# Chunks 2 to 21 of a chunked linear-attention kernel put in the order of a list schedule made at build time

## The chip, the cores and the metric

The kernel runs on one NeuronCore of a Trainium2 chip. The metric is the device time of one execution in microseconds (us); the time given for a kernel is the median of its runs. The engines are called PE (TensorE; PEld is its weight load), DVE (VectorE), ACT (ScalarE), POOL (GpSimd) and SP (SyncE, which here only issues DMAs). Each engine works off its own instructions in the order in which the program holds them; between engines there are semaphore waits, which the framework sets wherever two instructions touch the same data.

## The reference

For each of 4 x 8 heads a 40x40 state is carried over 768 steps, and its output, 3072 tokens of 320 numbers, goes through a mixture of experts with a skip gate:

```
for t in range(S):
    y[:, :, t] = einsum('bhd,bhde->bhe', rt, state)
    Sa = einsum('bhde,bhe->bhd', state, at)
    state_decay = state * wt[:, :, None, :] - einsum('bhd,bhe->bhde', Sa, bt)
    state = state_decay + einsum('bhd,bhe->bhde', vt, kt)
...
do_compute = x @ w_skip > 0                  # other tokens: out = x
e_idx = argmax(xc @ w_gate); gate_w = softmax(...)[e_idx]
out[do_compute] = xc + gate_w * (relu(xc @ w1[e]) @ w2[e])
```

## The kernel before

The sequence is cut into 24 chunks of 32 steps. The 32 heads lie in two halves, x = 0 and x = 1, of 16 heads each. Within a chunk the recurrence is solved with matrices; between chunks only the 40x40 states are carried. The chunk loop in `attn` writes out, for each chunk c, the steps below in an order made by hand, and PE, ACT and DVE keep that order (`tc.manual_schedule`); POOL and SP are ordered by the framework, except in the prologue, where POOL is kept too.

The chain from chunk to chunk, for each half x, is:

- `rs` (L288): 16 small matmuls of r with the state, copied out by DVE (L292, even chunks) or ACT (L293, odd ones);
- `ux` (L302): matmuls of the chunk's decayed a with R1, copied to `UXs` by ACT (L304);
- `uq` (L313): matmuls with the inverse `TB`, four ACT copies into R1 (L315), and a mask on POOL (L317);
- `sst` (L325, L330): two sets of matmuls that make the new state and its transpose, copied by DVE (L334) or ACT (L335), and ACT (L338).

Beside the chain stand:

- `yy` (L348): the chunk's output, scaled by DVE into `XS` (L352) and stored twice by SP (L353);
- the preparation of later chunks, in units of a pair of chunks h. The scans on DVE (L114, L126, L119), products on POOL (L143, L151), the matrices in `m1` (L163: PE; L165: ACT copy; L174: DVE transpose; L170: POOL mask; L172: four DMAs on SP), and the transposes `kbt` (L185, L188), `wtt` (L197, L199) and `m2` (L207, L209);
- `tinv`, the inverse of 32x32 triangles for the next four chunks: 30 steps of two products (L228) and two subtractions (L230) on DVE, half of them on a block that lies in PSUM (`px`), then an ACT copy (L232) and a DVE transpose into `TB` (L235). `T()` puts one or two of its steps between the other steps of a chunk;
- the routing of the finished tokens (`route`), two chunks at a time: transposes on PE (L628), ACT copies (L630), scores (L636, L637), a row of small DVE operations (L644 to L681) with one exponential on ACT between L646 and L653, and scattered stores on POOL (L684). `RP(...)` says at which places of a chunk it goes on one step;
- the loads on SP of w, a, k/b and v (L94, L97, L100, L107) and on POOL of r/v (L104).

Scans, `m1` and `tinv` run in chunks 0 to 19; chunks 20 to 23 only finish. The loads of the experts' weights begin in chunk 20, the experts themselves follow the last chunk.

The eight PSUM banks are dealt out in fixed rings: two banks `pc` (for `rs`, `ux`, `uq`), two `ps` (`sst`), two `pq` (all preparation and routing), one `py` (`yy`), one `px` (`tinv`). A ring gives its banks in turn:

```
    def tile(s,shape,dt,tag=None,name=None):
        t=s.t[s.n%len(s.t)]; s.n+=1
```

Of the kernel before, what the change touches and what calls it, by code (L numbers as in the profile page):

```python
# [19 lines left out]
def host(r,k,v,w,a,b,moe_w_skip,moe_w_gate,moe_w1,moe_w2):  # L20
# [16 lines left out]
    o.update(raw_r=r,raw_k=k,raw_v=v,raw_w=w,raw_a=a,raw_b=b)  # L37
    o.update(moe_host(moe_w_skip,moe_w_gate,moe_w1,moe_w2))
    return o
class Ring:  # L40

    def __init__(s,pool,n,k):
        s.t=[pool.tile([128,512],F32,name=f"{n}{q}") for q in range(k)]; s.n=0
    @classmethod
    def of(c,t):
        r=c.__new__(c); r.t=t; r.n=0
        return r
    def tile(s,shape,dt,tag=None,name=None):
# [9 lines left out]
def attn(ctx,tc,i,m,out,X):  # L58
    nc=tc.nc; NPH=6
    ov=out.rearrange("(b c t) f -> c b t f",b=4,t=32); Xv=X.rearrange("(b c t) f -> c b t f",b=4,t=32)  # L60
    P=lambda n,b,**k: ctx.enter_context(tc.tile_pool(name=n,bufs=b,**k))
    cp=P("const",1); wk=P("wk",1); wk2=P("wk2",2); wk3=P("wk3",3); wk4=P("wk4",4)
# [297 lines left out]
    if 1:  # L360
# [248 lines left out]
KT=((0,128),(128,256),(256,320))  # L609
class Moe:  # L610
    def __init__(s,ctx,tc,i,out,cp):
        s.tc,s.nc,s.i,s.out=tc,tc.nc,i,out; s.ctx=ctx
        nc=tc.nc
        dr=ctx.enter_context(tc.tile_pool(name="dr",bufs=1,space=DRAM))
        s.xg=dr.tile([E_*CAP,XW],F32,name="xg")
        s.X=dr.tile([3072,DM],F32,name="X")
        s.mc=cp.tile([128,552],F32,name="mc")
        s.wg=cp.tile([128,3,9],F32,name="wg")
        tz=s.mc[:,488:552]; s.mT=bass.AP(tz.tensor,tz.offset+31,(tuple(tz.ap[0]),(-1,32),(1,32))); s.mQ=s.mc[:,32:64]; s.idn=s.mc[:,64:192]; s.tri=s.mc[:,192:320]; s.one=s.mc[:,320:448]
        s.e8=s.mc[:,448:456]; s.base0=s.mc[:,456:464]; s.tok=s.mc[:,464:488]  # L620
        s.base=s.base0; s.WH,s.WL={},{}
# [226 lines left out]
                V.tensor_tensor(S,S,g,ALU.add)  # L848
            for b in range(4): nc.sync.dma_start(xv[b][:,ds(t0,U),:],y[8*b:8*b+8])
def dense_moe(m,X):  # L850
    tc,nc=m.tc,m.nc; V=nc.vector
    with tc.tile_pool(name="gw",bufs=1) as wp, tc.tile_pool(name="gps",bufs=1,space=PSUM) as gps:
        m.ps,m.wk=gps,wp
        with tc.For_i(0,3072,128) as r0:
# [12 lines left out]
                V.copy_predicated(acc,mk,y)  # L867
            nc.sync.dma_start(m.out[ds(r0,128),:],acc)
def general(m,fi,raw,X):
    tc,nc=m.tc,m.nc  # L870
    fa=nc.values_load(fi[0:1,2:3],min_val=0,max_val=1)
    fw=nc.values_load(fi[0:1,0:1],min_val=0,max_val=1)
    with tc.If(fa>0):
        with tc.If(fw>0):
            seq_attn(tc,raw,X)
        dense_moe(m,X)

def build(tc,i,out):
    with ExitStack() as ctx:
# [8 lines left out]
        with tc.manual_schedule(engines={ET.PE,ET.Activation,ET.DVE}), P("pp",1,space=PSUM) as m.pp, P("rt",1) as m.wk, P("xp",2) as m.xp:  # L888
# [16 lines left out]
```

## Time and profile before

| | us |
|---|---|
| median of 3 runs (666.47 to 667.10) | 666.92 |
| the profiled execution | 663.83 |
| its span, first to last instruction | 662.1 |
| chunk 2's first `rs` to chunk 22's first `rs` | 97.16 to 487.45 |
| start of the experts' steady part (stage from 530) to the end | 132 |

Times within the trace count from the start of the span. The stages of the prediction are cut at the first `rs` matmul (L288) of chunks 2, 4, 8, 12, 16, 20 and 22. In a row of the timeline stand start, duration, engine, line, operation, `output<-input`, shapes, a count, and in brackets the engine's idle time ahead of it and the instruction that ended it. In a list of waits stand who waited for whom, the total in us, how often, and the longest.

### The profile page before, as it was taken

The page shows a single profiled execution, that of the slowest core. Times are in us where ns is not written, and L with a number is a line of the kernel's source. Part 1 is how long each engine was busy: PE and PEld are TensorE (multiplying, and loading weights), DVE is VectorE, ACT ScalarE, POOL GpSimd, SP SyncE. Part 2 cuts the span into 40 slices and gives each one's busy share as a digit, 9 for nine tenths or more (in the row PEclk, how much of TensorE's full clock was granted, in tenths as well). Part 3 has the DMA queues.
Part 4 walks back from the last instruction along what each step waited for, and adds up shares of the span by engine and source line. Part 5 has one row for each costly group of instructions (what it writes and reads, how often), then busy time and mean ns, then how long its engine had stood idle before and what let it go on. Part 6 is the DMA issues. An engine that isn't in the chain of part 4 may idle for free.

```text
span 662.1 us, 33508 instructions
## 1 busy us (share of the span) xinstructions
PE 515.5 (78%) x14772; PEld 432.2 (65%) x14772; DVE 489.7 (74%) x1182; ACT 419.5 (63%) x1151; POOL 324.2 (49%) x246
## 2 busy tenths in 40 slices
PE   4777776676776787767785877878886899999995
PEld 1543456565664576656664666666775599999995
DVE  7998697858997479973999736864166457888881
ACT  5463674586965778567785677887885354555540
POOL 5481951648545375553946442223132155666661
PEclk8786895799977898878889689988788999999998
DMA  7473665352443525335253333453365266676210
GB/s 227 152 242 107 166 207 160 104 177 63 139 125 107 174 63 150 109 112 168 83 156 88 107 113 81 140 153 113 105 178 167 73 183 201 214 229 216 77 48 24
DMA packets 67446, 91.06 MB, mean 138 GB/s; under 512 B 32564, under 2 KB 54657, under 8 KB 65806
## 3 DMA queue, kind: packets, MB, share of 16 engines
q1 hardware_dynamic: 62350, 74.05, 38.1%
q0 software_dynamic: 4944, 14.80, 6.6%
q8 instruction: 118, 1.93, 1.2%
q14 instruction: 34, 0.28, 0.1%
HBM read 74.03 MB, written 17.08 MB: 138 GB/s over the span
## 4 chain that ended last, share of the span: by engine, by line
PE 24%; DVE 11%; ACT 8%; issue 5%; DMA 2%; POOL 1%; SPq 0%; POOLq 0%; DVEq 0%; ACTq 0%
PE pc L782 5%; PE ps L793 4%; PE px L782 3%; ACT R1t L315 2%; PE py L793 2%; ACT L2t L188 2%; DVE M L228 2%; PE ps L325 2%; DVE ti L789 2%; PE pc L313 1%; PE pc L288 1%; DVE M L230 1%; PE ps L330 1%; ACT SS L338 1%; ACT R1t L209 1%
## 5 line engine op out<-in xcount | busy, mean ns | idle before, releaser
L317 POOL TENSOR_TENSOR R1t<-R1t,mc 64x512 f32<-64x512 f32 x46 | 60.5, 1315 | 104.7 <-ACT R1t L315 72.6
L315 ACT COPY R1t<-pc 32x288 f32<-32x288 f32 x192 | 74.9, 390 | 20.7 <-PE pc L313 17.6
L730 POOL TENSOR_TENSOR WL<-WR,WH 128x1280 fp32r<-128x1280 f32 (+1 forms) x21 | 57.7, 2782 | 8.7 <-ACT WH L729 8.6
L188 ACT COPY L2t<-pq 64x160 f32<-64x160 f32 x184 | 52.8, 287 | 7.5 <-PE pq L185 5.1
L684 POOL DMA_INDIRECT xg<-XS,ix x24 | 25.5, 1064 | 64.3 <-DMA xg<-XS,ix 26.0
L325 PE MATMUL ps<-R1t,L2t 128*40 128x40 f32 x1472 | 48.2, 221 | 11.0 <-issue 5.3
L143 POOL TENSOR_TENSOR WR<-WR,M 128x1024 f32<-128x1024 f32 (+1 forms) x19 | 44.2, 2332 | 25.8 <-DVE M L114 19.7
L228 DVE TENSOR_TENSOR M<-M 128x22 f32<-128x22 f32 (+10 forms) x110 | 55.0, 500 | 0.0
L325 PEld LDWEIGHTS ps<-R1t,L2t 128*40 128x40 f32 x1472 | 39.3, 132 | 18.9 <-ACT R1t L315 8.9
L338 ACT COPY SS<-ps 40x320 f32<-40x320 f32 x92 | 38.7, 420 | 19.9 <-PE ps L330 18.5
L209 ACT COPY R1t<-pq 32x128 f32<-32x128 f32 x184 | 47.2, 256 | 5.5 <-PE pq L207 1.3
L288 PE MATMUL pc<-rvt,SS 128*40 128x32 f32 x1472 | 44.9, 216 | 7.2 <-issue 4.8
L288 PEld LDWEIGHTS pc<-rvt,SS 128*40 128x40 f32 x1472 | 38.3, 135 | 15.4 <-issue 7.8
L330 PE MATMUL ps<-L2t,R1t 128*40 128x40 f32 x1472 | 42.9, 218 | 6.5 <-issue 6.4
L313 PE MATMUL pc<-UXs,TB 32*32 32x72 f32 x1536 | 43.1, 255 | 6.0 <-issue 5.9
L330 PEld LDWEIGHTS ps<-L2t,R1t 128*40 128x40 f32 x1472 | 38.2, 134 | 7.3 <-issue 7.2
L230 DVE TENSOR_TENSOR M<-M 128x22 f32<-128x22 f32 (+10 forms) x110 | 40.8, 371 | 0.0
L230 DVE TENSOR_TENSOR px<-px,M 128x168 f32<-128x168 f32 (+8 forms) x150 | 39.1, 260 | 1.4
L729 ACT CAST WH<-WR 128x1024 fp32r<-128x1024 f32 (+1 forms) x35 | 39.6, 1132 | 0.0
L313 PEld LDWEIGHTS pc<-UXs,TB 32*32 32x32 f32 x1536 | 32.1, 122 | 11.4 <-issue 8.9
L789 DVE CAST ti<-xe 128x2 int32<-128x2 f32 x8 | 39.3, 4911 | 0.2
L174 DVE STREAM_TRANSPOSE M<-pq 128x128 f32<-128x128 f32 x40 | 12.1, 308 | 36.9 <-ACT M L165 24.3
(240 smaller groups left out, 1529.3 us busy)
## 6 DMA issues: line engine op xcount, KB each, us to landing
rvt<-rv POOLq DMA_DIRECT2D x21, 512.0 KB, 3.9
WR<-kb SPq DMA_DIRECT2D x10, 1024.0 KB
WR<-w SPq DMA_DIRECT2D x16, 640.0 KB
WR<-w SPq DMA_DIRECT2D x16, 512.0 KB
M<-wt SPq DMA_DIRECT2D x9, 520.5 KB
M<-at SPq DMA_DIRECT2D x8, 512.0 KB
WR<-w SPq DMA_DIRECT2D x16, 256.0 KB
R1t<-vt SPq DMA_DIRECT2D x48, 80.0 KB
```

Source lines behind the costliest of these rows:

```text
L188: A.copy(L2[x][h%NL2][64-64*x:128-64*x,c,bb*4:bb*4+4,:],pt[64*c:64*c+64,:,64*x:64*x+40])
L209: A.copy(R1[x][c%NR1][ao[x]:ao[x]+32,4*b:4*b+4,40:72],Pp[32*b:32*b+32])
L228: V.tensor_tensor(tv,NLt[:,j,j+1:32].unsqueeze(2).broadcast_to([128,n,k]),X[:,j,lo:hi].unsqueeze(1).broadcast_to([128,n,k]),ALU.mult)
L230: for tv,xv in q: V.tensor_tensor(xv,xv,tv,ALU.subtract)
L288: TE.matmul(RS[s,v,:],SS[x][:,b//2,v,:],rr[:,b%2,2*hh+x,:],start=True,stop=True)
L313: TE.matmul(UQ[q,hh,:],Tb[q,x*8+hh*2+c%2,:],UXd[x][q,hh,:],start=True,stop=True)
L315: A.copy(R[uu,4*b:4*b+4,:],UQ[32*b:32*b+32,:,:])
L317: (V if c==NC-1 else G).tensor_tensor(R[pq,:,40:72],R[pq,:,40:72],mQ[pq].unsqueeze(1).broadcast_to([64,16,32]),ALU.mult)
L325: TE.matmul(ST[s,v,:],l2[:,cc,u,:],R[:,u,0:40],start=True,stop=True)
L330: TE.matmul(S2[s,v,:],R[:,u,0:40],l2[:,cc,u,:],start=True,stop=True)
L730: def low(s,E,o,x,h): E.tensor_tensor(s.R(o),x,h,ALU.subtract)
L782: for n,(a,b) in enumerate(mm): TE.matmul(ph[:,g],R(a),R(b),start=n==0,stop=n==7)
```

## The change

All engines are wrapped (`Eng`, `Rec`). From chunk 2 on (`rec.on=True`) no instruction is issued; each call is kept as a task, with the data that it reads and writes (down to the partition quarter and the element), a cost in us from a formula by engine and size, and a latency for DMAs. Consecutive matmuls into one PSUM tile are one task. At chunk 22 `rec.flush()` finds the dependences, makes a list schedule of all tasks of chunks 2 to 21 on DVE, ACT, POOL, PE and SP, and issues the tasks by their planned start. POOL's order is kept in that stretch as well. The list takes, on each engine, the task with the smallest key (place in the old order less the weighted length of the work that hangs on it) among those that are ready, unless another one fits in before it.

The six banks of `pq`, `pc` and `ps` become one stock: a tile in PSUM gets its bank in the plan. The two banks `ps` are kept for `sst` and for the oldest tile that waits. Of the banks that are free in time the plan takes the one that became free last. `py` and `px` stay as they are. Small tiles that a pool gave out in turn become fixed tiles in turn with the same number of buffers (`Static`).

What is computed, the number of instructions of each engine and the code of one chunk are the same; chunks 0, 1, 22 and 23, the prologue and the experts are issued as before. The other edits touch the fallback path for unusual inputs, which does not run.

The core of the diff:

```
+class Rec:
+    HOP=0.12; PW=1.25
+    def cost(s,e,op,w,r,a):
+        n=max(sz(x) for x in (w[:1]+r[:1]))
+        if 'dma' in op:
+            by=4*n*min(128,w[0].ap[0][1])
+            return (0.06 if e=='S' else 1.0 if 'ind' in op else 0.6),2.0+by/2.6e5
+        if e=='P': return (0.145 if op=='transpose' else max(0.0005*sz(w[0]),0.058)),0
+        if e=='A': return 0.15+0.00085*n,0
+        if e=='G': return (0.08+n*0.0008 if op=='memset' else 0.65+0.0015*n),0
...
+        if op=='tensor_tensor': return 0.14+0.00105*n*(1 if ps else 1.6),0
...
+    def plan(s,keep=False):
...
+                av=[(at[k],k) for k in at if at[k] is not None and k not in got.values() and (k not in s.rest or o==old[0] or s.first[o] in s.rest)]
+                if not av: return None
+                a=max(min(av)[0],free[T[i].e],rdy[i])
+                a,k=max(x for x in av if x[0]<=a)
...
+                c.sort(key=lambda x:s.key[x[1]])
+                x=c[0]
+                while True:
+                    f=[y for y in c if y[0]<x[0] and y[0]+T[y[1]].d<=x[0]+s.LET]
+                    if not f: break
+                    x=f[0]
...
+    def keys(s):
+        w=max(sum(t.d for t in s.tasks if t.e==e) for e in 'VAGP')/len(s.tasks)
+        s.key=[i*w-s.FAR*t.up for i,t in enumerate(s.tasks)]
...
-    ps_c,ps_s,ps_y,ps_p,ps_x=(Ring(pp,n,k) for n,k in (("pc",2),("ps",2),("py",1),("pq",2),("px",1))); m.ps=ps_p
+    rec.banks={t.name:t for t in PQ+PC+PS}; rec.rest=[t.name for t in PS]
+    ps_c,ps_s,ps_p=(Ring(t,rec) for t in (PC,PS,PQ)); ps_y,ps_x=Ring(PY),Ring(PX); m.ps=ps_p
...
+            if c==2: rec.on=True
             if c==20: m.load(0)
             if c==22:
+                with tc.manual_schedule(engines={ET.Pool}): rec.flush()
```

Two places of the engines' orders follow. The changed kernel issues everything from one helper, so that its rows have one line number, L209; the operands tell what a row is. Banks are numbered: pq, pc and ps have two each, and the numbers behind the names differ between the two kernels.

**DVE, chunk 11, the end of the third inversion.** `M<-M,px` and `px<-px,M` are the last steps of `tinv`, `XS<-py` the output of a chunk, `TB<-M` the transpose that ends the inversion, `R1t<-ps` the new state. Before:

```order
L228 TENSOR_TENSOR M<-M,px_106 128x8
L230 TENSOR_TENSOR px_106<-px_106,M 128x8
L352 TENSOR_TENSOR XS<-py_103,WT 128x320
L235 STREAM_TRANSPOSE TB<-M 128x32x2x2x8
L334 TENSOR_TENSOR R1t<-ps_102,D_2599 40x8x40 x2
```

And now:

```order
L209 TENSOR_TENSOR M<-M,px_106 128x8
L209 STREAM_TRANSPOSE M<-pc_101 128x4x32
L209 TENSOR_TENSOR px_106<-px_106,M 128x8
L209 STREAM_TRANSPOSE M<-ps_103 128x4x32
L209 STREAM_TRANSPOSE M<-pq_99 128x4x32
L209 STREAM_TRANSPOSE M<-ps_104 128x4x32
L209 MEMSET M 128x17
L209 TENSOR_TENSOR XS_1345<-py_105,WT_478 128x320
L209 STREAM_TRANSPOSE TB<-M 128x32x2x2x8
L209 SCALAR_TENSOR_TENSOR M<-M 128x1041
```

Three transposes of `m1` and a memset, which belong to other work, now stand with the output's product between the last subtraction and the transpose into `TB`; with the one ahead of them the transposes empty four different banks.

**PE, chunks 2 and 3, around the routing's transposes.** `pq<-WR` (32x64) is `m1`, `mc,XS` the routing's transpose of a chunk's output, `rvt,SS` is `rs`, `UX,TB` is `uq`, `R1t,WR` or `R1t,M` is `ux`, `rvt` alone `m2`, `L2t,R1t` and `R1t,L2t` (40x40) are `sst`. Before:

```order
L163 MATMUL pq_104<-WR 32x64 x16
L302 MATMUL pc_99<-R1t,M 32x72 x16
L207 MATMUL pq_105<-rvt 32x32 x16
L628 MATMUL pq_104<-mc,XS 128x128 x2
L628 MATMUL pq_104<-mc,XS 64x128
L288 MATMUL pc_100<-rvt,SS_116 40x32 x16
```

And now:

```order
L209 MATMUL pq_99<-WR 32x64 x16
L209 MATMUL pc_102<-UX_451,TB 32x72 x16
L209 MATMUL pq_100<-rvt_150,SS_116 40x32 x16
L209 MATMUL pc_101<-WR 32x64 x16
L209 MATMUL pc_102<-rvt_150 32x32 x16
L209 MATMUL ps_104<-mc,XS_1344 128x128 x2
L209 MATMUL ps_104<-mc,XS_1344 64x128
L209 MATMUL pq_100<-WR 32x64 x16
L209 MATMUL ps_103<-L2t,R1t 40x40 x16
L209 MATMUL pc_102<-R1t,WR 32x72 x16
L209 MATMUL ps_104<-wg,xT_1466 32x9 x12
L209 MATMUL pc_102<-R1t,L2t 40x40 x16
```

Before, the routing's transpose went into the bank that an `m1` two groups ahead had filled; now it takes a bank that no `m1` holds, two such products stay in banks of their own, and one bank (`pc_102`) is filled four times in eleven rows.

More of the change, by code (lines that the diff above doesn't have):

```diff
@@ L39, in host, with __init__, __getattr__, tile @@
     return o
+class Task:
+    __slots__=("e","op","calls","R","W","d","lat","out","p","n","pr","al","up")
+class Eng:
+    def __init__(s,rec,e,real): s.rec,s.e,s.real=rec,e,real
+    def __getattr__(s,op):
+        fn=getattr(s.real,op)
+        return lambda *a,**k: s.rec.call(s.e,op,fn,a,k)
+class Shim: pass
+class Static:
+    def __init__(s,pool,bufs): s.pool,s.bufs,s.r=pool,bufs,{}
+    def tile(s,shape,dt,tag=None,name=None,bufs=None):
+        t=tag or name; n=int(np.prod(shape[1:]))
+        if t not in s.r: s.r[t]=[[s.pool.tile([128,n],dt,name=f"{t}{q}") for q in range(bufs or s.bufs)],0]
+        r=s.r[t]; x=r[0][r[1]%len(r[0])][0:shape[0],0:n]; r[1]+=1
+        if len(shape)==2: return x
+        ax=["abcd"[q] for q in range(len(shape)-1)]
+        return x.rearrange("p ("+" ".join(ax)+") -> p "+" ".join(ax),**{a:v for a,v in zip(ax,shape[1:])})
@@ L40, with __init__, of @@
 class Ring:
-    def __init__(s,pool,n,k):
-        s.t=[pool.tile([128,512],F32,name=f"{n}{q}") for q in range(k)]; s.n=0
+    def __init__(s,t,rec=None): s.t=t; s.n=0; s.rec=rec
     @classmethod
-    def of(c,t):
-        r=c.__new__(c); r.t=t; r.n=0
-        return r
+    def of(c,t,rec=None): return c(t,rec)
     def tile(s,shape,dt,tag=None,name=None):
         t=s.t[s.n%len(s.t)]; s.n+=1
+        if s.rec: s.rec.bank(t)
         n=int(np.prod(shape[1:]))
@@ L60, in attn @@
     ov=out.rearrange("(b c t) f -> c b t f",b=4,t=32); Xv=X.rearrange("(b c t) f -> c b t f",b=4,t=32)
-    P=lambda n,b,**k: ctx.enter_context(tc.tile_pool(name=n,bufs=b,**k))
-    cp=P("const",1); wk=P("wk",1); wk2=P("wk2",2); wk3=P("wk3",3); wk4=P("wk4",4)
+    P=lambda n,b,**k: Static(ctx.enter_context(tc.tile_pool(name=n,bufs=1,**k)),b)
+    rec=m.rec; nc=rec.shim
+    cp=P("const",1).pool; wk=P("wk",1); wk2=P("wk2",2); wk3=P("wk3",3); wk4=P("wk4",4)
     pp=m.pp
-    ps_c,ps_s,ps_y,ps_p,ps_x=(Ring(pp,n,k) for n,k in (("pc",2),("ps",2),("py",1),("pq",2),("px",1))); m.ps=ps_p
+    bk=lambda n,k: [pp.tile([128,512],F32,name=f"{n}{q}") for q in range(k)]
+    PQ,PC,PS,PY,PX=bk("pq",2),bk("pc",2),bk("ps",2),bk("py",1),bk("px",1)
+    rec.banks={t.name:t for t in PQ+PC+PS}; rec.rest=[t.name for t in PS]
+    ps_c,ps_s,ps_p=(Ring(t,rec) for t in (PC,PS,PQ)); ps_y,ps_x=Ring(PY),Ring(PX); m.ps=ps_p
     V,A,G,TE,SP=nc.vector,nc.scalar,nc.gpsimd,nc.tensor,nc.sync
@@ L611, in __init__ @@
     def __init__(s,ctx,tc,i,out,cp):
-        s.tc,s.nc,s.i,s.out=tc,tc.nc,i,out; s.ctx=ctx
+        s.rec=Rec(tc.nc); s.tc,s.nc,s.i,s.out=tc,s.rec.shim,i,out; s.ctx=ctx
         nc=tc.nc
@@ L850, in dense_moe @@
 def dense_moe(m,X):
-    tc,nc=m.tc,m.nc; V=nc.vector
+    m.nc=m.tc.nc; tc,nc=m.tc,m.nc; V=nc.vector
     with tc.tile_pool(name="gw",bufs=1) as wp, tc.tile_pool(name="gps",bufs=1,space=PSUM) as gps:
@@ L869, in general @@
 def general(m,fi,raw,X):
-    tc,nc=m.tc,m.nc
+    tc,nc=m.tc,m.tc.nc
     fa=nc.values_load(fi[0:1,2:3],min_val=0,max_val=1)
@@ L887, in build @@
         P=lambda n,b,**k: tc.tile_pool(name=n,bufs=b,**k)
-        with tc.manual_schedule(engines={ET.PE,ET.Activation,ET.DVE}), P("pp",1,space=PSUM) as m.pp, P("rt",1) as m.wk, P("xp",2) as m.xp:
+        with tc.manual_schedule(engines={ET.PE,ET.Activation,ET.DVE}), P("pp",1,space=PSUM) as m.pp, P("rt",1) as rt, P("xp",1) as xp:
+            m.wk,m.xp=Static(rt,1),Static(xp,2)
             with ExitStack() as c2: attn(c2,tc,i,m,out,m.X)
```

122 lines of the change are left out of this document (added).

## The prediction

> **What bounds the kernel now.** I read the page first, for what ends last:
>
> ```profile
> span 662.1 us, 33508 instructions
> PE 515.5 (78%) x14772; PEld 432.2 (65%) x14772; DVE 489.7 (74%) x1182; ACT 419.5 (63%) x1151; POOL 324.2 (49%) x246
> PE 24%; DVE 11%; ACT 8%; issue 5%; DMA 2%; POOL 1%; SPq 0%; POOLq 0%; DVEq 0%; ACTq 0%
> ```
>
> No engine is full, and the chain goes through three of them. A mean over the span mixes stages, so the busy times of the stages come next, cut at the first `rs` matmul of chunks 2, 4, 8, 12, 16, 20 and 22:
>
> ```profile
> core 0: us, PE busy (x) PEld busy (x) DVE busy (x) ACT busy (x) POOL busy (x), PEclk, DMA share, GB/s
> 0.00:97.16 97.16, 66.26 (x1789) 41.60 (x1789) 83.61 (x132) 54.20 (x146) 57.59 (x50) 0.84 0.59 179
> 97.16:143.86 46.70, 32.72 (x1188) 27.71 (x1179) 36.38 (x110) 29.20 (x90) 20.79 (x17) 0.78 0.47 143
> 143.86:224.14 80.28, 57.76 (x2245) 47.58 (x2236) 66.10 (x184) 57.82 (x176) 45.66 (x36) 0.89 0.42 123
> 224.14:305.95 81.81, 60.72 (x2247) 50.42 (x2237) 64.10 (x184) 57.80 (x176) 43.26 (x36) 0.85 0.42 120
> 305.95:386.91 80.96, 60.26 (x2245) 49.72 (x2236) 65.54 (x184) 57.73 (x176) 45.75 (x36) 0.87 0.42 125
> 386.91:454.84 67.93, 52.78 (x2119) 44.45 (x2109) 43.44 (x170) 53.79 (x164) 18.09 (x18) 0.92 0.42 121
> 454.84:487.45 32.61, 28.12 (x1004) 23.49 (x995) 7.26 (x28) 27.13 (x83) 8.37 (x8) 0.84 0.39 116
> 530.00:662.00 132.00, 123.19 (x936) 121.31 (x936) 96.16 (x108) 60.33 (x81) 73.42 (x37) 0.98 0.48 149
> ```
>
> The changed stretch is 97.16 to 487.45, 390.29 us for 20 chunks. DVE is the busiest engine up to chunk 15, ACT in chunks 16 to 19, PE in 20 and 21, with shares of 78, 82, 78, 81, 79 and 86%. The busiest engines' times add up to 36.38 + 66.10 + 64.10 + 65.54 + 53.79 + 28.12 = 314.03 us, or 80.5% of the stretch. The other 76 us are waits in an order made by hand. Which ones, the waits of DVE in the stretch tell:
>
> ```profile
> DVE M L174 <- ACT M L165: 24.3, 8, 6.4
> DVE mx L644 <- ACT sc L637: 21.8, 6, 9.3
> DVE TB L235 <- ACT M L232: 13.9, 5, 3.0
> DVE sm L653 <- ACT ex L647: 10.8, 7, 3.1
> ```
>
> These 70.8 us are of one kind: an instruction for later use (a transpose of `m1`, a routing step, the end of an inversion) stands at the head of the queue before its input is there, and what is behind it could run. Two examples from the timeline:
>
> ```profile
> 302.99 1.97 DVE L235 STREAM_TRANSPOSE TB<-M 128x1024 f32<-128x1024 f32 x1 [2.84 <-ACT M L232]
> 314.58 0.32 DVE L174 STREAM_TRANSPOSE M<-pq 128x128 f32<-128x128 f32 x1 [5.23 <-ACT M L165]
> ```
>
> PE has the same through the banks. Here, in the timeline, the routing's transpose waits until DVE empties the bank of an `m1`:
>
> ```profile
> 125.71 0.90 PE L628 MATMUL pq<-mc,XS 128*128 128x128 f32 x3 [4.14 <-DVE M L174]
> ```
>
> And in the waits of PE over the stretch the same wait and two others for a bank of that ring:
>
> ```profile
> PE pq L628 <- DVE M L174: 12.3, 5, 4.1
> PE pq L207 <- ACT L2t L188: 10.8, 9, 1.4
> PE pq L185 <- ACT L2t L188: 5.2, 8, 1.6
> ```
>
> **The change part by part.** *The order.* No computing instruction is added or taken away: by the two orders each engine has as many as before (PE 8327, DVE 1316, ACT 1192, POOL 270, SP 400). So busy times stay, and only waits can change. At the first place shown in the change, the inversion's last transpose has three other transposes and a memset between it and its input; at the second, the routing's transpose no longer shares a bank with an `m1`. Both waits quoted from there should shrink or go.
>
> How full can the busiest engine get? From below, the nearest row is chunks 20 and 21: the same steps in the same in-order queues, with little preparation between them, PE at 28.12 of 32.61, 86.2%; the prologue's DVE is at 83.61 of 97.16, 86.1%. From above, the experts' part, with long matmuls and few handovers, has PE at 123.19 of 132.00, 93.3%. I take 86.2%, as the work there is that of the stretch. Then it takes 314.03 / 0.862 = 364.3 us instead of 390.29: **26.0 us less**. Of this 20.5 come from chunks 2 to 15 (289.75 to 232.12 / 0.862 = 269.3), 5.5 from chunks 16 to 19 (67.93 to 62.4), none from the last two. 20.5 us is about a third of DVE's 57.6 idle us in its stages. At 93.3% the stretch would take 336.6, 53.7 less. What is late next, once DVE no longer waits on transposes, is the chain itself: in chunks 20 and 21, with DVE at 22%, a chunk still took 16.3 us, against 20.1 in the full stages.
>
> *The banks.* The plan takes, of the free banks, the one that became free last. Counting groups of matmuls in the two orders, a bank is filled again by the second or third group after it 184 times now, 78 times before: 106 close reuses more, some five a chunk. Each is planned to be free just in time, so an ACT or DVE copy that is late by the prices holds PE up although another bank is free, and behind that matmul the whole PE queue. One wait of this kind costs 5.2 / 8 = 0.65 us in the `L185` row and 10.8 / 9 = 1.2 us in the `L207` row. Against it stand the 12.3 us of the `L628` row. I take zero for the balance, keep 12 us of gain at one end, and at the other all 106 at 0.65 us, a loss of 69 us if every one lay on the path. Most should not, since the plan's prices are near the trace for ACT; a copy of 320 columns is priced 0.15 + 0.00085 x 320 = 0.42 us, and the page has it at 420 ns:
>
> ```profile
> L338 ACT COPY SS<-ps 40x320 f32<-40x320 f32 x92 | 38.7, 420 | 19.9 <-PE ps L330 18.5
> ```
>
> The Trainium skill speaks against this choice of bank: "Perfetto Trace Analysis", section Matmuls, says that independent groups should rotate through different PSUM banks, so that emptying one overlaps the next group's matmuls. By it the close reuses would be lost time, and the sum would be the slower case below; the row that bears it out so far is `L185`, 0.65 us where two groups share a ring of two.
>
> *POOL and SP.* POOL's rows move with the rest: r/v loads, masks, products. POOL is at most 57% busy in a stage of the stretch, and most of its waiting is for work that comes late, not for room:
>
> ```profile
> POOL R1t L317 <- ACT R1t L315: 72.6, 28, 6.9
> ```
>
> So nothing is taken for it. On SP the plan prices an issue at 0.06 us, and here is what one takes:
>
> ```profile
> L107 SPq DMA_DIRECT2D R1t<-vt x48: 560/606/1087, 7.9 to 493.0; - x48
> ```
>
> The chain of waits has one landing of such a load:
>
> ```profile
> 493.04 2.54 DMA R1t<-vt
> ```
>
> A load of v behind three stores is then 4 x 0.6 + 2.54 = 5 us after its `yy` instead of the planned 2.4. By the orders, `yy` of a chunk and the `ux` that needs that load are 21 to 24 PE rows apart, before 25 to 26, about one chunk each time, so 14 us or more cover it. Cost zero; uncovered it would be 2.6 us a chunk and half, 100 us in all, so a plan that let the two come close would show at once.
>
> *Small edits.* Fixed tiles instead of pools keep the number of buffers: zero. At the seams, chunk 2's start finds DVE still in chunk 1's work, which the plan doesn't know, and chunk 22 begins behind the plan's leftovers (masks, outputs, routing). Both are bounded by half a chunk, 8.2 us, either way, since leftovers can also run ahead; I take zero.
>
> The sum: 663.83 - 26.0 = 637.8 against the profiled execution, which stands 3.1 us below the median of the runs; so **640.9** on the median's scale. About 0.2%, 1.3 us, is what a measurement of this kernel can tell from no change.
>
> **The rivals.** *Fuller still (613):* the plan reaches across stages and brings the busiest engine to the experts' 93.3%: 666.92 - 53.7. For it: DVE's idle time in its stages is 57.6 us, and 70.8 us of waits have one cure. Against it: the steps here are 0.2 to 2 us long with a handover after each.
>
> *The waits move (656):* only the waits at the inversion's end go, and the others come back under other names, since a step's input is late whatever stands before it. Of 13.9 us in five waits four lie where DVE is busiest: 11.1 us. For it: the routing's `sm` waits on ACT's exponential two instructions on.
>
> *The close banks make it slower (682):* at 0.65 us a wait, the gain of 26 us is eaten when 40 of the 106 close reuses, two a chunk, hold up the path. With 64 of them it is 41.4 us, or 666.92 - 26.0 + 41.4. For it: DVE's real times scatter far more than any formula, as the next rows show. Against it: the old order paid such waits too, and PE has gaps to take some.
>
> *POOL holds DVE up more (683):* a product of DVE with both inputs outside PSUM stands still while POOL works:
>
> ```profile
> 167.85 1.28 POOL L317 TENSOR_TENSOR R1t<-R1t,mc 64x512 f32<-64x512 f32 x1 [0.82 <-ACT R1t L315]
> 167.88 1.34 DVE L228 TENSOR_TENSOR M<-M 128x60 f32<-128x60 f32 x1
> 169.30 0.20 DVE L230 TENSOR_TENSOR M<-M 128x60 f32<-128x60 f32 x1
> ```
>
> The groups of the stretch:
>
> ```profile
> L228 DVE TENSOR_TENSOR M<-M 128x120 f32<-128x120 f32 (+10 forms) x103 | 52.7, 512 | 0.0
> L230 DVE TENSOR_TENSOR M<-M 128x112 f32<-128x112 f32 (+10 forms) x104 | 39.5, 380 | 0.0
> L228 DVE TENSOR_TENSOR M<-M,px 128x184 f32<-128x184 f32 (+9 forms) x143 | 35.2, 246 | 1.6
> ```
>
> Against the 246 ns of the form with an input in PSUM, the stretch loses 103 x 0.266 + 104 x 0.134 = 41 us so. The plan only prices such an operation 1.6 times up and lets it meet POOL. In chunks 4 to 15 DVE would have to grow by 22 us over its 195.74 to undo the gain there and in the rest (243.05 + 10.0 = 253.05, times 0.862 = 218.1); if it grew by 36 us, so that today's loss nearly doubled, it would take 231.7 / 0.862 = 268.8 there, and the whole 682.7. Against it: POOL's operations are as many as before. "SBUF — State Buffer" in the Trainium skill, section Who interferes with whom, gives the rule: of a DVE instruction with two SBUF inputs and a GpSimd instruction that reads SBUF, one fully blocks the other. The trace agrees, 1.34 us beside POOL's 1.28 against 0.20.
>
> *Nothing happens (667):* the plan keeps much the same weave of steps, and the chain pays as before.
>
> **How the numbers follow.** The forecast has 0.48, with a range of its own from 632 to 652. Fuller 0.17, waits move 0.12, close banks 0.13, POOL 0.05, nothing 0.05. Faster is forecast, fuller and waits move: 0.77; same 0.05; slower 0.13 + 0.05 = 0.18. The range goes from 613, the fuller case, to 668, just past no change; it leaves out the two slower cases, 0.18, and the little below 613.
>
> **What would show it.** Right: the first `rs` of chunk 2 to that of chunk 22 takes near 364 us; DVE is at 86% in chunks 4 to 15; the waits `M L174 <- ACT M L165`, `TB <- ACT M` and PE's wait of the routing's transpose for DVE are mostly gone; busy times of each engine in the stretch, found by operand, are as before. Close banks: PE's waits for ACT copies of another kind of step rise by more than 26 us. POOL: the mean of the 128x60 to 128x130 products rises well over 512 and 380 ns. Wrong altogether: a stretch over 390 us with PE or ACT waiting on DMAs of v or on DVE's copies of the state.

## The result, and the profile after

The changed kernel is slower: 672.60 us in the median of 6 runs (670.4 to 674.24) against 666.82 (664.49 to 668.43), a ratio of 1.011 (1.008 to 1.014; ratios and intervals are the recorded ones, and need not equal the quotient of the two medians). The forecast was 640.9. The profiled execution took 672.7 us with a span of 670.5. Its busy times in the same stages, cut at the first `rs` of chunks 2, 4, 8, 12, 16, 20 and 22, and in the last row for the whole stretch:

```profile
core 0: us, PE busy (x) PEld busy (x) DVE busy (x) ACT busy (x) POOL busy (x), PEclk, DMA share, GB/s
97.52:143.40 45.88, 33.08 (x1129) 28.20 (x1123) 41.49 (x106) 27.73 (x83) 19.75 (x20) 0.70 0.42 123
143.40:229.41 86.01, 60.55 (x2242) 51.16 (x2237) 71.19 (x185) 58.56 (x175) 44.31 (x38) 0.82 0.40 121
229.41:312.87 83.46, 63.42 (x2244) 53.17 (x2236) 65.57 (x184) 58.28 (x175) 43.42 (x36) 0.80 0.40 119
312.87:391.81 78.94, 58.59 (x2244) 48.72 (x2236) 63.77 (x182) 57.59 (x174) 40.47 (x32) 0.89 0.39 117
391.81:463.06 71.25, 55.46 (x2128) 46.34 (x2129) 49.67 (x186) 54.13 (x166) 19.03 (x18) 0.90 0.41 120
463.06:495.50 32.44, 27.18 (x999) 22.60 (x999) 8.18 (x27) 27.85 (x85) 9.33 (x9) 0.89 0.44 130
97.52:495.50 397.98, 298.28 (x10962) 250.19 (x10957) 299.88 (x867) 284.14 (x855) 176.32 (x152) 0.84 0.41 121
```

The stretch takes 397.98 us, 7.7 more than before; what lies around it grew by 0.7 (670.5 - 397.98 = 272.5 against 271.8). DVE shows it in two numbers. It was busy 282.82 us and idle 107.5; now it is busy 299.88 and idle 98.1. The list does take away waiting, 9.4 us of it, but DVE works 17.1 us longer on the same instructions. PE, with the same matmuls, is busy 5.9 us longer, at a granted clock of 0.84 instead of 0.87.

The list of DVE's waits in the stretch shows which waits are left:

```profile
DVE R1t L209 <- PE pq L209: 24.8, 10, 4.5
DVE XS L209 <- PE py L209: 18.1, 6, 4.9
DVE mx L209 <- ACT sc L209: 7.9, 5, 5.8
DVE base L209 <- PE pc L209: 6.6, 2, 6.0
DVE R1t L209 <- PE ps L209: 4.7, 3, 3.2
DVE R1t L209 <- ACT WE L209: 4.5, 1, 4.5
DVE R1t L209 <- PE pc L209: 4.3, 4, 1.7
DVE sm L209 <- ACT ex L209: 4.1, 5, 1.5
DVE M L209 <- ACT M L209: 3.7, 3, 1.8
```

The four waits of before, 70.8 us, are down to 7.9 + 4.1 + 3.7 = 15.7, and the wait of the inversion's last transpose has gone altogether. PE's wait of the routing's transpose for DVE, 12.3 us before, is gone too. In their place DVE waits for PE: for the products that it takes into `R1t`, 24.8 + 4.7 + 4.3 us, and for a chunk's output (`XS<-py`), 18.1. Of before the same list had

```profile
DVE R1t L334 <- PE ps L325: 7.9, 4, 4.1
...
DVE XS L352 <- PE py L348: 4.3, 6, 1.7
```

ACT waits for PE's products too, and for a load of w that it never waited for in the stretch before, as its waits show:

```profile
ACT R1t L209 <- PE pq L209: 30.6, 24, 3.8
ACT R1t L209 <- PE pc L209: 24.5, 19, 3.9
ACT junk L209 <- DMA M<-wt: 12.5, 3, 5.3
```

What such a wait does behind it is plainest at 170 us. First SP in the timeline, where the load of w (`M<-wt`) is issued at 170.13, behind four copies of `M` into `WR` that had to wait for POOL's product that began at 163.76 us:

```profile
166.54 3.48 SPq L209 DMA_DIRECT2D WR<-M  x4
170.13 0.53 SPq L209 DMA_DIRECT2D M<-wt  x1
```

Then ACT, where `junk<-M,wc` is the check that looks over the input w:

```profile
175.66 0.72 ACT L209 ACTIVATE junk<-M,wc 128x512 bf16<-128x512 f32 x1 [5.33 <-DMA M<-wt]
...
177.35 0.78 ACT L209 COPY R1t<-pq 32x288 f32<-32x288 f32 x2
```

And PE:

```profile
179.75 0.66 PE L209 MATMUL pq<-rvt 40*32 40x32 f32 x32 [7.10 <-ACT R1t L209]
```

The check belongs to work for a later chunk, but it heads ACT's queue for 5.33 us. The copies of `R1t` stand behind it, and PE stands still for 7.10 us. It is a wait of the kind that the change set out to remove, made new at another place.

Where DVE's 17 us come from is read from its groups by line. Here are the products `M<-M` of the inversion, the scans and the product with a mask into `px`:

```profile
L209 DVE TENSOR_TENSOR M<-M 128x130 f32<-128x130 f32 (+10 forms) x202 | 88.5, 438 | 1.9
L209 DVE TENSOR_TENSOR_SCAN M<-M 128x1041 f32<-128x1041 f32 (+1 forms) x14 | 39.8, 2840 | 0.4
...
L209 DVE TENSOR_TENSOR px<-M,mc 128x256 f32<-128x256 f32 x4 | 8.2, 2044 | 0.1
```

In the groups of before, by form, the scans and the product into `px` were shorter:

```profile
L114 DVE TENSOR_TENSOR_SCAN M<-M 128x1041 f32<-128x1041 f32 x7 | 16.8, 2396 | 0.6
L126 DVE TENSOR_TENSOR_SCAN M<-M 128x1040 f32<-128x1040 f32 x7 | 16.5, 2352 | 0.0
...
L216 DVE TENSOR_TENSOR px<-M,mc 128x256 f32<-128x256 f32 x4 | 4.0, 1009 | 0.1
```

The products `M<-M` have not changed (438 ns each, and (52.7 + 39.5) / 207 = 445 before). The scans cost 39.8 - 33.3 = 6.5 us more and `px<-M,mc` 4.2 more. The other groups moved both ways (the routing's `eq<-sc,mx` fell from 8.9 to 1.7 us) and add 1.3: by form, all groups add up to 337.7 us against 325.7, 12.0 more. The last 5.1 of the 17.1 us are overlap between DVE's instructions that the list gave up; they are told with the table of the lists below. Why the scans and `px<-M,mc` are longer, the timeline shows. POOL at 161 to 167 us:

```profile
161.64 2.15 POOL L209 TENSOR_TENSOR WR<-WR,M 128x1024 f32<-128x1024 f32 x1
163.76 2.75 POOL L209 TENSOR_TENSOR M<-M,mc 128x256 f32<-128x256 f32 x1
```

DVE beside it:

```profile
161.70 4.28 DVE L209 TENSOR_TENSOR_SCAN M<-M 128x1040 f32<-128x1040 f32 x1
...
167.16 4.38 DVE L209 TENSOR_TENSOR px<-M,mc 128x256 f32<-128x256 f32 x1
```

A scan that took 2.35 us in the mean of before lasts 4.28 beside POOL's products, and a `px<-M,mc`, 1.01 in the mean of before, lasts 4.38. The list can put them there because its formula gives each engine a time of its own.

So three readings stood at the outset. *Heads of queues*: wrong prices (a load's too low, a small matmul's too high) put steps at the head of a queue before their input is there. *Banks*: the newest free bank makes PE wait. *POOL*: its products stand beside DVE's long instructions.

### The profile page after: what moved, and what is told of

Read it like the earlier page. It is cut to its first block, busy times and chain, and to the rows that moved or that the text cites. A ratio compares the mean times of both kernels' runs of the same rounds, so it can differ in the third digit from the quotient of the medians.

```text
span 670.5 us, 33450 instructions
## 1 busy us (share of the span) xinstructions
PE 524.7 (78%) x14772; PEld 442.8 (66%) x14772; DVE 505.2 (75%) x1182; ACT 421.5 (63%) x1151; POOL 319.2 (48%) x246
## 5 line engine op out<-in xcount | busy, mean ns | idle before, releaser
L209 ACT COPY R1t<-pq 32x128 f32<-32x128 f32 (+3 forms) x244 | 79.6, 326 | 33.8 <-PE pq L209 30.6
L209 DVE TENSOR_TENSOR M<-M 128x130 f32<-128x130 f32 (+10 forms) x202 | 88.5, 438 | 1.9
L209 POOL TENSOR_TENSOR R1t<-R1t,mc 64x512 f32<-64x512 f32 x40 | 57.3, 1431 | 67.8 <-ACT R1t L209 46.5
L209 ACT COPY R1t<-pc 32x288 f32<-32x288 f32 (+3 forms) x140 | 49.1, 351 | 26.2 <-PE pc L209 24.5
L209 POOL TENSOR_TENSOR WR<-WR,M 128x1024 f32<-128x1024 f32 x14 | 30.3, 2167 | 27.9 <-DMA WR<-kb 24.0
L209 DVE TENSOR_TENSOR_SCAN M<-M 128x1041 f32<-128x1041 f32 (+1 forms) x14 | 39.8, 2840 | 0.4
L209 POOL DMA_DIRECT2D rvt<-rv x20 | 12.0, 600 | 58.8 <-PE pc L209 32.0
L209 DVE TENSOR_TENSOR px<-px,M 128x168 f32<-128x168 f32 (+8 forms) x141 | 36.9, 262 | 2.6
L209 POOL DMA_INDIRECT xg<-XS,ix x20 | 21.0, 1052 | 35.0 <-DMA xg<-XS,ix 15.9
L209 DVE TENSOR_TENSOR R1t<-pq,D 40x256 f32<-40x256 f32 (+1 forms) x34 | 15.0, 441 | 29.8 <-PE pq L209 24.8
L109 POOL DMA_INDIRECT out<-ro,ti x16 | 15.7, 983 | 45.4 <-PE pq L109 21.6
L209 DVE TENSOR_TENSOR M<-M,px 128x168 f32<-128x168 f32 (+8 forms) x141 | 34.9, 248 | 1.5
L109 PE MATMUL pc<-xH,WH 128*128 128x256 f32 x126 | 32.5, 283 | 0.1
L209 PE MATMUL pq<-rvt 40*32 40x32 f32 x928 | 16.0, 210 | 20.7 <-ACT R1t L209 12.0
L209 PE MATMUL py<-L2t,R1t 128*32 128x40 f32 x1280 | 24.0, 222 | 9.7 <-issue 9.3
L109 DVE TENSOR_TENSOR WL<-WR,WH 128x1024 fp32r<-128x1024 f32 (+1 forms) x19 | 24.5, 1291 | 8.1 <-ACT WH L109 7.6
L209 PE MATMUL pq<-rvt,SS 128*40 128x32 f32 x736 | 21.1, 213 | 11.6 <-DVE M L209 5.4
L209 ACT COPY L2t<-pc 64x160 f32<-64x160 f32 x100 | 28.6, 286 | 2.4 <-PE pc L209 0.6
```

The lines of the kernel that those rows point to most:

```text
L109: if not s.on: return fn(*a,**k)
L209: for fn,a,k,own in s.tasks[i].calls: fn(*[at(x,own) for x in a],**{n:at(x,own) for n,x in k.items()})
```

## The experiments

All ratios are against the kernel before on the same chip, with 95% intervals. "Stretch" is chunk 2's first `rs` to chunk 22's in the one profiled execution of a run; it scatters by about 1% and is read with the ratio.

**First four: one cause each.** The check of w later on ACT:

```
+        for i,t in enumerate(s.tasks):
...
+            s.st[i]=max(s.st[i],min(s.st[i]+8.0,nx-0.01))
```

> The planned order of the changed kernel, with one thing moved: the check of w on ACT (the Square activation that reads a freshly loaded w) is issued 8 us of plan later, as long as the next load into the same buffer allows; nothing else moves. Late inputs at the head of a queue: the three waits of ACT for the load of w, 12.5 us in the profile of the changed kernel, go, and with them 8 to 12 us: 661 to 665 us. Close banks: no change, 671 to 674. POOL holding up DVE: no change, 671 to 674.

668.54 us, 1.006 (1.002 to 1.010). ACT's wait for w is gone, but ACT still waits 34.5 and 25.6 us for PE's products. Of the 1.1% loss about half came back, but the two intervals overlap, so that this is not clear of noise.

The banks, in the same order, given out by longest free:

```
+                k=min(c)[1]; s.bank_of[o]=k; at[k]=b[o]
...
+        s.rebank()
```

> The planned order unchanged, but each PSUM tile gets, of the banks that the plan has free, the one that became free first instead of last. Close banks: at least half of the loss against the rivals' ground goes, 660 to 667 us. Late inputs: PE waits a little less, 670 to 673. POOL holding up DVE: no change, 671 to 674.

669.65 us, 1.006 (1.003 to 1.010). About half a per cent better, again with overlapping intervals; the stretch is 396.17. DVE is busy 299.91 us, as under the change, yet not in the same instructions: the scans are at 34.4 us and `px<-M,mc` at 3.8, near their times before, and the products `M<-M` at 98.6 instead of 91.7. Which of them pays changes though the order is the same.

The old order with the stock of banks and the recorded stretch:

```
-        s.deps(); s.keys(); s.plan()
+        s.deps(); s.keys(); s.plan(True)
```

> The stock of six banks, the newest free one first, and the recorded stretch as in the changed kernel, but every engine keeps the old order of its instructions. Close banks: as slow as the changed kernel or slower, 671 to 690 us. Late inputs made by the new order: as the kernel before, 664 to 669. POOL holding up DVE: as the kernel before, 664 to 669, if its loss came with the new order.

671.86 us, 1.013 (1.008 to 1.017). The old order does not bring the old time back: something else in the change costs as much as all of the loss.

A lower price for a small matmul:

```
-        ... max(0.0005*sz(w[0]),0.058)
+        ... max(0.0005*sz(w[0]),0.045)
```

> A list schedule again, with one price changed: a small matmul costs 0.045 us in the plan instead of 0.058, so that PE's tasks add up to about what PE is busy in the trace of the kernel before. Late inputs: the plan no longer takes PE for the one full engine, places copies and products by their own weight, and gains something, 655 to 668 us. Close banks: the plan is tighter, more just-in-time reuse, 672 to 685. POOL holding up DVE: 668 to 676, since the products meet POOL as before.

666.63 us, 1.002 (0.997 to 1.006): even with before.

**Next four: what is left of the change when the order is old, and prices together.** Old order, and each tile only in its old bank:

```
+ s.plan(True);  av=[... if k==s.first[o]]
```

> The stretch is recorded and emitted at one place as in the changed kernel, POOL kept in the recorded order, tiles fixed, but each engine keeps its old order (chunk by chunk, as written) and each PSUM tile its old bank of its own pair. Nothing of the list and nothing of the stock of banks is left; what remains is the recording, the fixed tiles and POOL's kept order. If the recording costs nothing (my prediction took the small edits at zero), the time is that of the kernel before, 666 +-2. If the 1.3 per cent that the old order with the stock of banks lost came from the stock, this run is at the kernel before and that one stays 7 us above it. If it came from the fixed tiles or from POOL's order, this run shows the same 671 to 674 with the old banks.

671.29 us, 1.009 (1.005 to 1.013). Neither the list nor the stock is left in this kernel, and yet it has most of the loss.

Old order, the stock, the longest free bank:

```
-                a,k=max(x for x in av if x[0]<=a)
+                a,k=min(x for x in av if x[0]<=a)
```

> The old order on each engine, banks from the stock of six, but a tile takes the bank that has been free longest and not the one freed last. Theory 'close banks': a write soon behind the last reader of the same bank makes PE wait, so this run gives back most of the 7 us that the old order with the newest free bank lost: 664 to 668. Rival: the stock itself costs (three pairs that each kept their own distance are now shared, and a tile of the state's products can take the bank that a product of the next chunk would have had): then no difference to 671 to 673.

669.57 us, 1.010 (1.007 to 1.012). Newest, longest free or own bank: 1.013, 1.010, 1.009, all within each other's intervals. The choice of bank is not the cause.

The list with the lower price, and tiles kept to their old pairs:

```
+ av=[... if k[:2]==s.first[o][:2]]
```

> List order made with a small matmul at 0.045 in place of 0.058, and a tile takes only a bank of its own old pair. Theory 'the prices set the order': with the price corrected the kernel with the stock came out at 666.6, even with before; if the stock costs as well, the pairs bring it to 658 to 664, faster than before. Rival, that the stock frees the list to look ahead and the pairs bind it: 667 to 672.

694.26 us, 1.042 (1.034 to 1.051), against 1.002 with the stock. A miss for the theory: this list, bound to pairs, is 4% slower than with the stock. How the pairs cost it was not looked into.

Four corrections at once (matmul 0.045, an issue on SP 0.6 and 150 GB/s, longest free bank, check of w 8 us later):

> List order with the small matmul at 0.045, a DMA on SP's queue at 0.6 to issue (its median step in the rows is 0.61) and its bytes at 150 GB/s in place of 260, the bank that has been free longest, and the check of w on ACT put 8 us later. Theory 'late inputs at the head of a queue, from prices that are too low for loads': ACT's waits on the load of w and POOL's on the load of k go, and the four corrections together give 655 to 662. Rival 'the list order is worth nothing here because what ends its waits is the chain of one chunk and not the order': 664 to 668, with the waits only at other places.

664.58 us, 0.998 (0.995 to 1.002). DVE's stretch is 302.28 us busy and 87.0 idle: the waits shrink as the theory says, and the busy time stays up. The time misses the 655 to 662 that the theory gave and lies in the rival's range.

**Then: POOL's order, and a control.** As e5, with POOL left to the scheduler:

```
-                with tc.manual_schedule(engines={ET.Pool}): rec.flush()
+                rec.flush()
```

> The old order per engine with each tile's old bank, as in the run that came out at 671.29, but POOL is left to Tile's scheduler over the stretch, as in the kernel before: its rows are then those of before in the same order. Theory 'POOL's kept order costs 6 us': back at the kernel before, 664 to 667. Rival 'the fixed tiles cost it' (each buffer of a tag has its own place and a round of its own): stays at 670 to 672.

670.1 us against 671.4, 0.999 (0.996 to 1.002). This is the kernel before in fixed tiles, with POOL's rows in the old order, and it has the old time: tiles and recording cost nothing, and POOL's rows in the order as written cost about 1% between these two runs. POOL's waits suggest how; as written (e5), the routing's scatter `xg` stands ahead of products and waits for DVE:

```profile
POOL R1t L209 <- ACT R1t L209: 82.3, 17, 8.4
POOL xg L209 <- DVE R1t L209: 32.7, 7, 6.2
```

and left to the scheduler (e9):

```profile
POOL R1t L209 <- ACT R1t L209: 65.0, 22, 6.8
...
POOL xg L209 <- DVE R1t L209: 14.6, 4, 6.8
```

The 1% is seen in the times of the runs; the profiled executions of the two (stretch 391.07 and 392.50) don't show it, so its place is argued only.

The changed kernel with the same line undone:

> The changed kernel with one line undone: POOL is left to Tile's scheduler, the order of the list stays on DVE, ACT, PE (and in what is issued to SP). If POOL's order as given out is what costs 6 us, 664 to 668. Rival: the list's places for POOL fit the list's places for the others, and a POOL in another order makes DVE, PE and ACT wait for its products: 672 to 685.

678.1 us, 1.008 (1.005 to 1.011). Under the change's list, POOL's order is not what costs.

e8 with the same line undone:

> The list with the four corrections (664.58 before), POOL left to Tile's scheduler. If POOL's order costs 6 us whatever the list: 656 to 660, faster than before. If POOL's order belongs to the list: 665 to 680.

659.5 us, 0.983 (0.979 to 0.988): faster than both kernels, the best of the study. Freeing POOL, worth nothing under the change's list, takes this one from 0.998 to 0.983. In its stretch, in the row of the busy times, DVE's idle time is down to 85.3 us (380.26 - 294.95):

```profile
99.25:479.51 380.26, 292.01 (x10961) 246.12 (x10957) 294.95 (x869) 283.50 (x855) 175.96 (x153) 0.86 0.44 127
```

The control, a step between engines at 0.16 instead of 0.12:

```
-    HOP=0.12; PW=1.25
+    HOP=0.16; PW=1.25
```

> A control on how much of such differences is the luck of one list: the changed kernel with the price of a step between engines at 0.16 instead of 0.12, which no row speaks for more than the other. It moves hundreds of rows on each engine. If the lists of this kind all stand at +1.1 per cent, 671 to 674. If the order is brittle and what the prices did was chance, anywhere from 660 to 685.

672.51 us against 671.4, 1.001 (0.998 to 1.003). An edit that nothing speaks for gets back the whole loss. So a difference of 1% between two single lists proves nothing about the edit between them, and what e4 gave back can't be credited to its edit. In this list's one profile the scans are at 2.31 and 2.34 us in the mean and `px<-M,mc` at 0.82: without any rule for it, its scans met POOL less.

**Then: POOL's part, with lists that don't change.** 56 of POOL's products in the stretch, in place on `R1t` (40) and `M` (16), left out when the tasks are issued; the masks they apply are missing, the list is the same:

```
+            if s.tasks[i].e=='G' and ... and s.tasks[i].W[0] in s.tasks[i].R and ...: continue
```

> The changed kernel, its list and banks as they are, but POOL's 40 products in place on R1t and 16 on M in the stretch are left out when the list is given out (about 70 of POOL's 177 us; the masks they apply are missing). Theory 'POOL beside DVE ate the list's gain': DVE is busy 10 to 15 us less, and this run falls well below the old order without the same products: 645 to 655 against 660. Rival 'waits at other places, the order of one chunk's chain': both fall alike by a few us, and the list stays 4 to 8 us above the old order.

650.3 us, 0.976 (0.971 to 0.981).

> The old order with old banks and POOL left to the scheduler (the run that stood at 0.999 of before), the same 56 products of POOL left out. This is what the list without them is compared with. Theory 'POOL': 655 to 664, falling less than the list does. Rival: falls as much as the list or more, since POOL's product on R1t stands in the chain of a chunk between ACT's copy and PE.

652.14 us, 0.982 (0.975 to 0.990). The busy times in the stretch, of the list without them (e13):

```profile
100.27:472.94 372.67, 287.36 (x10963) 240.54 (x10957) 271.93 (x865) 285.09 (x855) 104.56 (x97) 0.89 0.44 129
```

Of the old order without them (e14):

```profile
98.68:474.40 375.72, 290.37 (x10998) 242.79 (x10989) 254.98 (x862) 283.82 (x860) 111.59 (x95) 0.87 0.44 130
```

And of the old order with them (e9):

```profile
98.74:491.24 392.50, 290.85 (x10997) 241.71 (x10989) 278.59 (x862) 282.78 (x860) 177.07 (x151) 0.88 0.43 124
```

The products cost the list 397.98 - 372.67 = 25.3 us and the old order 392.50 - 375.72 = 16.8. With them the list stands 1.2% above the old order (1.011 / 0.999), without them 0.6% below (0.976 / 0.982, which the intervals do not separate from none). So one and the same list loses to the old order with these products and does not lose without them. What the trial can't part is the two ways in which a product of POOL costs: beside DVE, and in a chunk's chain between ACT's copy and PE. DVE's busy time falls by 28.0 us in the list and by 23.6 in the old order, 4.3 more, where the stretch falls by 8.5 more; so time beside DVE is a part of it, and how large a part is not shown. Even without the products the list gains 3 us of stretch and not 26, and DVE is still busy 17 us longer than in the old order: 9.4 of this in longer instructions (the groups by form add up to 308.9 and 299.5 us; POOL's other work, 104.6 us, is still there), the rest in overlap.

Luck or not, e11's list with the price of the control:

> The list with the four corrections and POOL left to the scheduler (ratio 0.983), with the price of a step between engines at 0.16 instead of 0.12: a meaningless edit that moves rows all over the list. If the corrections and the free POOL make it, 0.978 to 0.988 again. If it was the luck of one list, anywhere from 0.985 to 1.01.

660.5 us, 0.993 (0.990 to 0.995). Faster again, by less than half as much; 0.993 is where the expectation put the luck of one list.

The corrected list, kept so that POOL's products and DVE's products and scans on SBUF never meet in the plan:

```
+        t.sh=e in 'VG' and ... not any('PSUM' in str(x.space).upper() for x in w+r) and op in ('tensor_tensor','tensor_tensor_scan')
...
+                    c.append((max(free[e],rdy[i],w[0],port if T[i].sh else 0.0),i,w[1]))
+            port=fin[i] if t.sh else port
```

> The list with the four corrections, POOL's order kept, and made so that a product or a copy product of POOL never stands beside a DVE product or scan that touches only SBUF. Theory 'POOL beside DVE': DVE's means of those groups fall towards their medians (scans 2.84 to 2.4 us, products on 128x126 below 0.5), busy time in the stretch falls by 8 us or more, and the time is 652 to 660. Rival, that the real times slide against the plan so that POOL and DVE meet anyway: busy time as before the edit (300 to 306) and 662 to 670.

657.95 us, 0.985 (0.978 to 0.992), where the same corrections without it gave 0.998. The scans are back in the groups by form:

```profile
L215 DVE TENSOR_TENSOR_SCAN M<-M 128x1040 f32<-128x1040 f32 x7 | 16.5, 2360 | 0.1
L215 DVE TENSOR_TENSOR_SCAN M<-M 128x1041 f32<-128x1041 f32 x7 | 16.3, 2329 | 0.1
```

Yet DVE's busy time fell by 3.1 us only (302.28 to 299.19), less than the 8 expected; why is told with the table.

**Last, the same edit alone, and once more with the control.**

> The changed kernel with one edit: the list keeps POOL's products and DVE's products and scans on SBUF apart in time; prices, banks and the check of w as in the change. If POOL beside DVE is what turned the gain into a loss: DVE's scans back to 2.35 us, DVE's busy time in the stretch 10 us or more below the change's 299.9, and 0.985 to 0.998 of the kernel before. If the loss is in the waits at other places: the scans shorten but the ratio stays at 1.005 to 1.012.

670.71 us against 668.29, 1.005 (1.001 to 1.008). On the change's own prices the edit gets back some of the loss and not all; by the expectation, 1.005 speaks for waits at other places. The scans are at 2.57 and 2.39 us. DVE is busy 294.75 us, 5.1 less, where 10 were expected.

> The list with the four corrections that keeps POOL and DVE apart (ratio 0.985), with the price of a step between engines at 0.16 instead of 0.12. If keeping them apart does it, 0.98 to 0.99 again. If it was the luck of one list, 0.99 to 1.005.

665.17 us against 668.29, 0.996 (0.993 to 0.999). This was expected if 0.985 was the luck of one list; the corrections without the rule, at the first step price, had 0.998. So a gain in time from keeping the two apart is not shown.

The lists side by side with the old order, from the profiled stretch of each:

| kernel | ratio | stretch | DVE busy | DVE idle | DVE, groups added up |
| --- | --- | --- | --- | --- | --- |
| before | 1 | 390.29 | 282.82 | 107.5 | 325.7 |
| old order, own banks, POOL free (e9) | 0.999 | 392.50 | 278.59 | 113.9 | 322.5 |
| the change | 1.011 | 397.98 | 299.88 | 98.1 | 337.7 |
| the change, other step price (e12) | 1.001 | 392.19 | 290.64 | 101.6 | 328.1 |
| the change, kept apart (e17) | 1.005 | 390.10 | 294.75 | 95.4 | 321.9 |
| corrections (e8) | 0.998 | 389.25 | 302.28 | 87.0 | 339.0 |
| corrections, POOL free (e11) | 0.983 | 380.26 | 294.95 | 85.3 | 332.1 |
| the same, other step price (e15) | 0.993 | 382.33 | 298.80 | 83.5 | 335.8 |
| corrections, kept apart (e16) | 0.985 | 383.70 | 299.19 | 84.5 | 321.6 |
| the same, other step price (e18) | 0.996 | 384.67 | 288.81 | 95.9 | 312.2 |

Every list here cuts DVE's idle time, the corrected ones by 12 to 24 us against before; every one also makes DVE busy longer, by 6 to 19 us. The five corrected lists stand at 0.983 to 0.998, those with the change's matmul and load prices at 1.001 to 1.011. That the corrections as a group are worth about 1% is likely from this; which of them is, stays open, since two lists that differ by the step price alone lie 0.9 to 1.1% apart.

The last column adds up DVE's groups by form, so that each instruction counts with its whole length. The sum exceeds the busy time, since an instruction can begin before the one ahead of it has ended. This overlap is 43 and 44 us in the old order, 37 to 38 in the lists and 22 to 27 in the lists kept apart. So keeping POOL apart did shorten DVE's instructions, by 17.4 us in e16 (339.0 to 321.6) and 15.8 in e17 (337.7 to 321.9), and lost 14.3 and 10.7 of it again in overlap. The timeline of before shows where overlap comes from:

```profile
126.70 0.21 DVE L228 TENSOR_TENSOR M<-M 128x60 f32<-128x60 f32 x1
126.83 0.24 DVE L230 TENSOR_TENSOR px<-px,M 128x88 f32<-128x88 f32 x1
126.99 0.20 DVE L230 TENSOR_TENSOR M<-M 128x60 f32<-128x60 f32 x1
127.12 0.23 DVE L228 TENSOR_TENSOR M<-M,px 128x80 f32<-128x80 f32 x1
```

The inversion's steps on its block in SBUF (`M<-M`) alternate here with those on its block in PSUM (`px`), which don't depend on them, and each begins 0.13 to 0.16 us after the one before, though it takes 0.20 to 0.24. Counted in the traces, steps of the two kinds stand side by side 364 times in the stretch before, 258 times in the change, 97 times in e17 and 50 times in e16. Two steps on the block in PSUM in a row, each of which needs the one before, don't overlap in any of these four. The hand order had woven the two blocks together, and the list, whose costs know no overlap, pulled them apart.

## Why the prediction was wrong

*"So busy times stay, and only waits can change."* This step failed first. The number of instructions stayed, the time of DVE's didn't: 282.82 to 299.88 us. Of these 17.1 us 10.7 are the scans and `px<-M,mc`, lengthened where they meet POOL, 1.3 the other groups together, and 5.1 overlap that the old order had. The busiest engines' times add up to 41.49 + 71.19 + 65.57 + 63.77 + 55.46 + 27.85 = 325.33 us instead of 314.03, 9.9 of the difference DVE's in chunks 2 to 15. At the 86.2% that I took, this alone is (325.33 - 314.03) / 0.862 = 13.1 us.

*"I take 86.2%."* This was the larger miss. The busiest engines reached 325.33 / 397.98 = 81.7%, up from 80.5, and DVE in chunks 4 to 15 is at 200.53 / 248.41 = 80.7% instead of 86. 397.98 - 325.33 / 0.862 = 20.6 us lie here. The row of chunks 20 and 21 was no model: there DVE has little to do, while over the stretch of the change PE, DVE and ACT are at 75, 75 and 71%. That a wait taken from one of three such engines comes back on another fits the new waits for PE; no run shows that nothing else sets the limit. The best list reached 294.95 / 380.26 = 77.6% on DVE over the stretch, where the change has 75.4 and before 72.5: so the direction of the forecast was there, and its size was 10 of 26 us even then.

*The waits that should go* went, 70.8 to 15.7 us. To read that as time saved was the slip; the rival "the waits move" had this, and priced it as a smaller gain, not as a loss.

*The banks at zero* held: three rules for the bank under the old order lie within 1.009 to 1.013. The rows had PE wait for ACT's copies of `R1t` for 17.3 + 5.8 us, but its longest, 7.10, is the check of w and no bank; the rise over before is under the 26 us that were to be the sign of close banks. The Trainium skill's rule in "Perfetto Trace Analysis", section Matmuls, to rotate through the banks, would have had the longest free bank ahead; the half a per cent or less that e2 and e6 show of it lies within their intervals. One list lost 4% without the stock (e7).

*POOL at zero* failed, and the rival that POOL holds DVE up more had the sign, with the wrong place. It looked to the mean of the products on 128x60 to 128x130, and that stood still (445 to 438 ns); in this execution the scans paid. It had asked for 36 us in chunks 4 to 15 to reach 683; there only 4.8 came (195.74 to 200.53), and 17 in the whole stretch, 5.1 of them no matter of POOL. What it left out is POOL's own order, which as written costs about 1% under the old order.

*SP at zero* failed in part: three loads of w came late to ACT's check for 12.5 us, through a queue that the plan thought ten times as fast as its rows. The cover I named, a chunk between `yy` and `ux`, was for loads of v, and held. *Small edits* at zero held (e9, 0.999).

*The range*, 613 to 668, left 0.18 for slower. Of the terms taken at zero, POOL and SP could cost much and gain little, and the sum gave them no share; the overlap of DVE's own instructions was not a term at all.

Open: which of the four corrections matters, where the 1% of POOL's written order lies, how much of POOL's price is paid beside DVE and how much in the chain, and what holds the busiest engines at 81.7%.

## What to carry to other kernels

A wait that a new order removes is not time saved until the profile shows what the engine does instead; cut the stretch into busy and idle time of the busiest engine, before and after, and a gain in idle time that is eaten by longer instructions is seen at once. A price list that gives each engine a time of its own is blind to two things that this kernel shows: what two engines hold against each other, and how neighbours on one engine overlap. A rule against the first cost most of its gain in the second, so add up the instructions' lengths beside the busy time. The prices of loads should be as the queue's rows have them; a load that comes late heads a queue like the waits that the order was to remove. And before a difference of 1% between two generated orders is put down to an edit, make an edit that means nothing and see how far that moves the time.

## What the runs showed of the hardware

DVE copies of two columns can stand still for as long as POOL works on products. In e17, where the plan no longer let products and scans meet POOL, the timeline of POOL at 203 us:

```profile
202.80 1.28 POOL L210 TENSOR_TENSOR R1t<-R1t,mc 64x512 f32<-64x512 f32 x1
204.04 2.17 POOL L210 TENSOR_TENSOR WR<-WR,M 128x1024 f32<-128x1024 f32 x1
```

And of DVE:

```profile
202.98 0.22 DVE L210 TENSOR_TENSOR px<-px,M 128x48 f32<-128x48 f32 x1
203.23 0.20 DVE L210 TENSOR_TENSOR M<-M,px 128x40 f32<-128x40 f32 x1
203.34 2.90 DVE L210 COPY XS<-mc 128x2 f32<-128x2 f32 x1
206.16 0.20 DVE L210 TENSOR_TENSOR px<-px,M 128x40 f32<-128x40 f32 x1
```

Products with an input in PSUM run beside POOL at 0.2 us. An output in PSUM is not enough: `px<-M,mc`, with both inputs in SBUF, took 4.38 us beside POOL in the change, and 10.0 us over its four instances in e17, 4.0 before, since the rule left out whatever touches PSUM. The copy of 128x2 from SBUF to SBUF, which takes 0.13 us alone in the same run, ends only when POOL's second product does, after 2.90; the change from POOL's first product to its second did not let it in. Over the ten copies this is 13.6 us instead of 1.9 before and 2.3 in the change: the plan of e17 held only products and scans apart. "SBUF — State Buffer" of the Trainium skill, section Who interferes with whom, says that a copy can take both ports and that of DVE and GpSimd the later one is then fully blocked. The row agrees as far as POOL's first product goes, which had begun ahead of the copy; that the copy, begun at 203.34, then also stood behind the second product, begun at 204.04, is not in that section. Scans are held up too, as the row of 4.28 us shows.

Neighbours on DVE that don't need each other overlap: in the rows of before at 126 us the next begins 0.13 to 0.16 us after the one ahead, with durations of 0.20 to 0.24. Where each needs the one before, as the two products at 202.98 and 203.23 above, it is 0.25 from start to start with durations of 0.22 and 0.20.

The granted clock was lower in the first half of the list's stretch: 0.70 in chunks 2 and 3 and 0.82 and 0.80 in chunks 4 to 11, where before had 0.78, 0.89 and 0.85, with 5.9 us more of PE's busy time on the same matmuls. It did not come with every list: e12 and e11 have 0.86 in the stretch, e9, in the old order, 0.88, and before 0.87.
